# Moving one of three bit steps of the float64 weights, and two small products of the attention, to ScalarE

## The chip, the cores and the metric

The kernel runs on one core of one Trainium2 chip. The metric is the device time of one execution in microseconds, as the median over runs. The engines are called by their names: TensorE (PE in the profile, its weight loads PEld), VectorE (DVE), ScalarE (ACT), GpSimd (POOL) and SyncE (SP, which issues the DMAs).

## The reference

Three parts follow each other: a linear attention with a decaying state, an MLP, and a mixture of experts with one expert per token.

```python
# attention: r, k, v, w (4, 8, 768, 48), u (8, 48)
for t in range(S):
    cur = np.einsum('bhd,bhe->bhde', u[None] * kt, vt)
    y[:, :, t] = np.einsum('bhd,bhde->bhe', rt, state + cur)
    state = wt[:, :, :, None] * state + np.einsum('bhd,bhe->bhde', kt, vt)
# MLP on x (3072, 384): w_in (384, 2048), w_out (2048, 384), both float64
h = x @ w_in
g = np.maximum(h, 0.0) + alpha * np.minimum(h, 0.0)
x = g @ w_out
# experts: argmax of x @ w_gate chooses one of 8
h = np.maximum(xe @ w1[e], 0.0)
out[mask] = gate_w[mask, None] * (h @ w2[e])
```

`w_in` and `w_out` come as float64: a float32 array divided by the square root of a float64 number. The kernel gets them as pairs of 32-bit words and makes float32 of them itself.

## The kernel before

The 3072 tokens are 24 tiles of 128 rows. Three tiles make a block, so there are 8 blocks. For each tile the attention makes `y`, transposed, straight into the MLP's input `xth` (high part) and `xtl` (what the high part leaves). The MLP goes through a block in 16 chunks of 128 of its 2048 columns: `p1` (line 611) multiplies a chunk of `w_in` with the block's `x`, ScalarE makes `gn` (614), VectorE `gt` (616), ScalarE `gh` (622), VectorE `gl` (624), and `p2` (637) multiplies by the chunk of `w_out` two steps later. Every product of the MLP is three matmuls, high by high, high by low and low by high; so each weight exists as `wih` and `wil` (or `woh` and `wol`).

**The weights.** There are 16 pieces, called weight 0 to 15 here; the even ones are of `w_in`, the odd ones of `w_out`, and weights 2g and 2g+1 serve chunks 2g and 2g+1. `wl_stages` makes each in four stages: `rebase` (216), where ScalarE copies the high word, read as a float32, with a scale of 2^-112 into `v64`; `words` (220 to 224), where VectorE shifts that three bits to the left, ors the top three bits of the low word in, and then the sign; `high` (237) on ScalarE and `low` (241) on VectorE. The tiles `raw` and `v64` have two buffers each; weight 2 lies in `spare`. The DMA of weight j+2 is issued on SyncE's queue after `words` of weight j.

**The attention of a tile.** VectorE scans the decays (`ex`, 291) and their inverses backwards (`rec`, 316) and multiplies `k` by them (333); GpSimd multiplies `r` by `ex` (306). TensorE makes the scores `pa` (371), ScalarE copies them to `at` (379), GpSimd masks them (383, two instructions). For the diagonal GpSimd makes `rk` in two products (338, 339), VectorE sums it into `c`, eight numbers per row (344), and GpSimd multiplies `c` with `v` into `cv`, two instructions (351). `cv` has one buffer for all tiles. TensorE transposes it into `px` (438), adds what the state (446, 449) and the scores (459) give, and ScalarE and VectorE make `xth` (464) and `xtl` (469) of it.

**The order.** Everything before the first `p1` is written out by hand: a table gives each step of tiles 0 to 2 and weights 0 to 2 a place (`PRO_OPS`, `PRO_MOVED`, `PRO_W`), and blocks of idle matmuls (`warm`, 161) are set between. From there on TensorE and GpSimd keep the written order, while the order on VectorE and ScalarE is made by a planner when the program is built. On every engine the queue runs strictly in its order: an instruction that waits holds up all behind it. Tiles 0 to 6 use the backward scan (`NBACK`); the attention of tiles 3, 4, 5 lies between the chunks of block 0.

Of the kernel before, what the change touches and what calls it, by code (L numbers as in the profile page):

```python
# [9 lines left out]
F32 = mybir.dt.float32  # L10
F32R = mybir.dt.float32r
BF16 = mybir.dt.bfloat16
I32 = mybir.dt.int32
U32 = mybir.dt.uint32
AF = mybir.ActivationFunctionType
ALU = mybir.AluOpType
AX = mybir.AxisListType
# [3 lines left out]
B, H, S, D = 4, 8, 768, 48  # L21
# [44 lines left out]
NSPE = 7  # L66

NBACK = 7

DMW = 2 * 512 + NP * 129 + 1  # L70

# [36 lines left out]
def attention_mlp_moe(ctx, tc, dmaj, tmaj, ub, alpha, w_in, w_out, w_gate, w_gate_b, wexp, out):  # L108
    nc = tc.nc
    vec, act, pool, pe, sp = nc.vector, nc.scalar, nc.gpsimd, nc.tensor, nc.sync  # L110
# [75 lines left out]
    raw_t, spare_t, wgb_t = {}, {}, {}  # L186
# [5 lines left out]
    def wl_dma(j):  # L192
        g, kind = j // 2, j % 2
        if j == 2:
            raw = spare_t[0][:, 1024:2560].bitcast(U32).rearrange("p (n c) -> p n c", c=2)
        else:
            raw = rp.tile([128, 768, 2], U32, tag="raw", name="raw")
        sp.dma_start(
            out=raw, in_=(w_in if kind == 0 else w_out)[g].bitcast(U32).rearrange("p (n c) -> p n c", c=2)
        )  # L200
# [6 lines left out]

    def wl_stages(j):

        g, kind = j // 2, j % 2  # L210
        q = g % 4
        cx = {}

        def rebase():
            cx["v"] = rp.tile([128, 768], F32, tag="v64", name="v64")
            act.activation(cx["v"], raw_t[j][:, :, 1].bitcast(F32), AF.Copy, scale=2.0**-112)

        def words():
            raw, vu = raw_t.pop(j), cx["v"].bitcast(U32)
            vec.tensor_scalar(vu, vu, 3, None, op0=ALU.logical_shift_left)  # L220
            vec.scalar_tensor_tensor(
                out=vu, in0=raw[:, :, 0], scalar=29, in1=vu, op0=ALU.logical_shift_right, op1=ALU.bitwise_or
            )
            vec.scalar_tensor_tensor(
                out=vu, in0=raw[:, :, 1], scalar=0x80000000, in1=vu, op0=ALU.bitwise_and, op1=ALU.bitwise_or
            )

        def parts():
            if kind == 0:
                sl = (slice(None), slice(None), slice(256 * q, 256 * q + 256))  # L230
                return wi_h[g // 4][sl], wi_l[g // 4][sl], cx["v"].rearrange("p (c f) -> p c f", c=KC)
            sl = (slice(None), slice(2 * q, 2 * q + 2))
            return wo_h[g // 4][sl], wo_l[g // 4][sl], cx["v"].rearrange("p (c d) -> p c d", c=2)

        def high():
            hi, _, v = parts()
            act.copy(hi, v)

        def low():
            hi, lo, v = parts()  # L240
            vec.tensor_tensor(out=lo, in0=v, in1=hi.bitcast(F32), op=ALU.subtract)  # L241

        return rebase, words, high, low

    tri = cst.tile([128, 128], BF16, name="tri")
# [33 lines left out]
    def att_tile(i, s0):  # L279
        cx = {}  # L280
        blk, j = divmod(i, NB)
# [6 lines left out]
        def scan():  # L288
# [13 lines left out]
            cx["v"] = tm_t[i][:, 2 * DM : 3 * DM]  # L302
            cx["rec"] = ap.tile([PR, NP, 129 if i < NBACK else 128], F32, tag="rec", name="rec", bufs=1)

# [3 lines left out]
        def rec(n):  # L308

            def at4(t, m):  # L310
                return t.rearrange("p a (g m) -> p a g m", m=4)[:, :, :, m]

            rc, ex = cx["rec"], cx["ex"][:, :, 1:129]
            if n == 0 and i < NBACK:
                vec.reciprocal(out=inj[:, :, 128], in_=ex[:, :, 127])
# [8 lines left out]
            elif n == 0:  # L324
                vec.reciprocal(out=at4(rc, 3), in_=at4(ex, 3))
            elif n == 1 and i < NBACK:
                return
# [19 lines left out]
        def diag_v():  # L347
            c, v = cx["c"], cx["v"].rearrange("p (a e) -> p a e", a=NP)
            cv = ap.tile([128, DM], F32, tag="cv", name="cv", bufs=1)
            for at, w, out in ((0, 32, cv[:, : 32 * H]), (64, 16, cv[:, 32 * H :])):  # L350
                pool.tensor_tensor(
                    out=out.rearrange("p (a m e) -> p a m e", a=NP, m=2),
                    in0=v[:, :, at : at + 2 * w].rearrange("p a (m e) -> p a m e", m=2),
                    in1=c.rearrange("p (a m o) -> p a m o", a=NP, o=1).to_broadcast([128, NP, 2, w]),
                    op=ALU.mult,
                )
            cx["cv"] = cv

        def decay():
            pm = ap.tile([PR, NP, 96], F32, tag="pm", name="pm", bufs=1)  # L360
            for p in range(NP):
                act.activation(pm[:, p, :], bmask[:, p, :], AF.Copy, scale=cx["ex"][:, p, 128:129])
            cx["pm"] = pm
# [102 lines left out]
        def x_low():  # L466
# [4 lines left out]
        ops = {  # L471
            "scan": scan, "r": decay_r, "rec0": lambda: rec(0), "rec1": lambda: rec(1), "k": lambda: rec(2),
            "rk": diag, "c": diag_sum, "cv": diag_v, "sc": scores,
            "a0": lambda: scores_out(0), "m0": lambda: mask(0), "a1": lambda: scores_out(1), "m1": lambda: mask(1),
            "yst": yst, "yav0": lambda: yav(0), "yav1": lambda: yav(1), "xh": x_out, "xl": x_low,
# [9 lines left out]
    def gate_block(blk, x2, g0):  # L485
# [39 lines left out]
        def bc(t):  # L525
            return t.to_broadcast([128, nt, E])
# [3 lines left out]
        def route():  # L530
# [15 lines left out]
            vec.tensor_tensor(out=sh, in0=l, in1=bc(m), op=ALU.subtract)  # L546
            act.activation(sh, sh, AF.Exp)
            cx.update(sh=sh, mi=mi, oh=oh, ac=ac)
# [53 lines left out]
    def p1(blk, f):  # L602
# [10 lines left out]
        gn = mp.tile([128, BN], F32, tag="gr", name="gn")  # L613
        act.activation(gn, ph, AF.Relu, scale=-1.0)  # L614
        gt = mp.tile([128, BN], F32, tag="gt", name="gt")
# [213 lines left out]
    def u_p1(u, f):  # L829
# [9 lines left out]
        gh = qp.tile([128, UNIT], F32R, tag="gh2", name="gh2", bufs=4)  # L839
        act.activation(gh, ph, AF.Relu)  # L840
        gl = qp.tile([128, UNIT], F32R, tag="gl2", name="gl2", bufs=4)
# [18 lines left out]
    def b_p1(u, q):  # L860
# [10 lines left out]
        hs = qp.tile([128, 256], F32, tag="hs", name="hs")  # L871
        act.activation(hs, ph, AF.Relu)
        d["hs", q] = hs
# [104 lines left out]
    for j in range(NWL):  # L978
        if j < len(PRO_W):
            s = [PT0 + t for t in PRO_W[j]]  # L980
        else:
            s = [2 * j - WL_OFF + n for n in range(4)]
        if j == NWL // 2:
            at_slot(s[0], lambda: w_tiles(1))
        for n, fn in enumerate(wl_stages(j)):
            at_slot(s[n], fn)
        if j and j + 2 < NWL:
            at_slot(s[1], lambda j=j: wl_dma(j + 2))
# [25 lines left out]
    for i in range(len(steps) + LAG):  # L1014
# [7 lines left out]
        if i < len(steps):  # L1022
            kind, b, f = steps[i]
# [6 lines left out]
        if i >= LAG:  # L1030
            kind, b, f = steps[i - LAG]
# [14 lines left out]
    with tc.For_i(0, nrem, 1) as iv:  # L1046
        tb = qp.tile([1, 1, 2], I32, tag="tb", name="tb", bufs=1)
        sp.dma_start(
            out=tb, in_=tabd[:, ds(iv * 2, 2)].rearrange("p (o c) -> p o c", o=1)
# [80 lines left out]
```

## Time and profile before

| | |
|---|---|
| median of 3 runs | 850.45 us (849.12 to 850.51) |
| the profiled execution, its own time | 848.63 us |
| its span, first to last instruction | 846.8 us |
| mean granted clock of TensorE, share of full speed | 0.985 |
| busy: TensorE, VectorE, ScalarE, GpSimd | 800.0, 611.5, 383.1, 306.6 us |

The time of an execution has 1.8 us around the span. Busy times are sums over the whole span and tell little of the first 130 us, where three engines share the attention, the weights and the MLP's first block. A row of the views names the source line, the engine and the operation, then the tile written and the tiles read; "idle before" is the time that the engine stood still ahead of it, and behind the arrow stands what ended that.

### The profile page before, as it was taken

Reading aid. Unit: us, or ns where it says so; the run is one execution under the profiler, and the core shown is the slowest. Engines: PE = TensorE matmul, PEld = TensorE weight load, DVE = VectorE, ACT = ScalarE, POOL = GpSimd, SP = SyncE. Lnnn points to the kernel's source line nnn. Section 1 sums busy time; section 2 is a strip of 40 time slices with the busy share of each in tenths; the row PEclk is TensorE's granted clock in tenths of the full one; section 3 lists DMA queues with packets and bytes.
Section 4 is the critical chain, followed back from the end, with each engine's and each line's share of the span. In section 5 each row is a group of like instructions: output and inputs, shape, how many; then the busy total and the mean of one; then the engine's idle time right before and its main releaser. Section 6 shows DMA issues by size and latency. Waiting matters only on the chain. (4 is left out here: it accounts for less than half of the span.)

```text
span 846.8 us, 15713 instructions
## 1 busy us (share of the span) xinstructions
PE 800.0 (94%) x6032; PEld 752.2 (89%) x6032; DVE 611.5 (72%) x1145; ACT 383.1 (45%) x730; POOL 306.6 (36%) x326
## 2 busy tenths in 40 slices
PE   6777999999999999999999999999899999999994
PEld 4567788999899999899999989989899999999993
DVE  5999995458958968967977953556856676767761
ACT  2465554334334243243343333355446566665641
POOL 6845562343324334334333431130433233223301
PEclk9889999999999999999999999999999999999998
DMA  9825652223123122124123200066277677686820
GB/s 284 256 87 205 216 179 96 66 69 96 38 96 69 63 70 86 46 70 124 35 68 96 67 2 29 2 242 214 95 254 250 216 239 256 229 299 200 297 95 20
DMA packets 30516, 114.80 MB, mean 136 GB/s; under 512 B 8229, under 2 KB 11592, under 8 KB 30440
## 3 DMA queue, kind: packets, MB, share of 16 engines
q1 hardware_dynamic: 26088, 103.53, 37.7%
q0 software_dynamic: 4352, 10.26, 3.2%
q8 instruction: 48, 0.79, 0.4%
q14 instruction: 28, 0.23, 0.1%
HBM read 104.11 MB, written 10.45 MB: 135 GB/s over the span
## 5 line engine op out<-in xcount | busy, mean ns | idle before, releaser
L611 PE MATMUL ph<-xth,wih 128*128 128x384 f32 x384 | 135.7, 353 | 13.6 <-DVE gt L616 10.3
L637 PE MATMUL py<-woh,gh 128*128 128x384 f32 x384 | 134.8, 351 | 1.7 <-DVE x L648 1.7
L611 PE MATMUL ph<-xth,wil 128*128 128x384 f32 x384 | 130.5, 340 | 3.7 <-DVE wil L241 3.7
L611 PE MATMUL ph<-xtl,wih 128*128 128x384 f32 x384 | 129.7, 338 | 0.1
L637 PE MATMUL py<-woh,gl 128*128 128x384 f32 x384 | 129.1, 336 | 0.0
L637 PE MATMUL py<-wol,gh 128*128 128x384 f32 x384 | 128.9, 336 | 0.0
L622 ACT CAST gh<-gt 128x384 fp32r<-128x384 f32 x128 | 65.7, 513 | 138.6 <-DVE gt L616 137.8
L616 DVE SCALAR_TENSOR_TENSOR gt<-gn,oma_s,ph 128x384 f32<-128x384 f32 x128 | 77.8, 608 | 54.6 <-ACT gn L614 54.4
L624 DVE TENSOR_TENSOR gl<-gt,gh 128x384 fp32r<-128x384 f32 x128 | 85.8, 670 | 30.6 <-ACT gh L622 28.3
L614 ACT ACTIVATE gn<-ph 128x384 f32<-128x384 f32 x128 | 62.4, 488 | 83.3 <-PE ph L611 80.1
L842 DVE SCALAR_TENSOR_TENSOR gl<-ph,gh 128x256 fp32r<-128x256 f32 x96 | 40.4, 422 | 73.3 <-ACT gh L840 73.1
L611 PEld LDWEIGHTS ph<-xth,wih 128*128 128x128 f32 x384 | 72.8, 189 | 20.7 <-DVE gt L616 13.0
L383 POOL TENSOR_SCALAR_AFFINE_SELECT at<-at 128x512 f32<-128x512 f32 x46 | 39.8, 884 | 124.0 <-ACT at L379 124.0
L512 DVE SCALAR_TENSOR_TENSOR sink<-x,wgb 128x384 f32<-128x384 f32 x120 | 82.8, 713 | 1.5 <-ACT x L648 1.2
L911 POOL DMA_INDIRECT out<-ys,meta x28 | 28.2, 1009 | 150.7 <-ACT ys L908 93.3
L837 PE MATMUL ph<-xh,w1h 128*128 128x256 f32 x288 | 81.2, 282 | 1.7 <-DVE gl L842 1.6
L837 PE MATMUL ph<-xh,w1l 128*128 128x256 f32 x288 | 80.9, 281 | 0.0
L837 PE MATMUL ph<-xl,w1h 128*128 128x256 f32 x288 | 80.3, 279 | 0.0
L637 PEld LDWEIGHTS py<-woh,gh 128*128 128x128 f32 x384 | 72.4, 189 | 7.9 <-issue 2.8
L611 PEld LDWEIGHTS ph<-xth,wil 128*128 128x128 f32 x384 | 72.9, 190 | 5.2 <-DVE wil L241 5.2
L611 PEld LDWEIGHTS ph<-xtl,wih 128*128 128x128 f32 x384 | 72.9, 190 | 0.4 <-DVE xtl L469 0.4
L637 PEld LDWEIGHTS py<-woh,gl 128*128 128x128 f32 x384 | 72.4, 188 | 0.6 <-DVE gl L624 0.6
(218 smaller groups left out, 1864.2 us busy)
## 6 DMA issues: line engine op xcount, KB each, us to landing
raw<-w SPq DMA_DIRECT2D x64, 768.0 KB, 5.0
tm<-tmaj SPq DMA_DIRECT2D x21, 704.0 KB, 4.3
dm<-dmaj SPq DMA_DIRECT2D x21, 674.2 KB, 4.9
raw<-w_out SPq DMA_DIRECT2D x8, 768.0 KB, 4.3
raw<-w_in SPq DMA_DIRECT2D x7, 768.0 KB, 4.8
x2d<-x SPq DMA_DIRECT2D x8, 576.0 KB, 4.0
both<-tmaj SPq DMA_DIRECT2D x3, 704.0 KB, 9.5
wgb<-w_gate_b SPq DMA_DIRECT2D x2, 768.0 KB, 4.4
```

Source lines behind the costliest of these rows:

```text
L383: pool.affine_select(out=cx[jj], in_=cx[jj], pattern=[[0, NP], [1, 128]], compare_op=ALU.is_gt, fill=0.0, base=0, channel_multiplier=-1,)
L512: vec.scalar_tensor_tensor(out=sink, in0=x2[:, j, :], scalar=1.0, in1=wgb_t[h][:, e, :], op0=ALU.mult, op1=ALU.mult, accum_out=cx["l"][:, ...
L611: pe.matmul(ph, lhsT=w, rhs=x[:, c, :], start=k == 0, stop=k == 3 * KC - 1)
L614: act.activation(gn, ph, AF.Relu, scale=-1.0)
L616: vec.scalar_tensor_tensor(out=gt, in0=gn, scalar=oma_s[:, f : f + 1], in1=ph, op0=ALU.mult, op1=ALU.add)
L622: act.copy(gh, gt)
L624: vec.tensor_tensor(out=gl, in0=gt, in1=gh.bitcast(F32), op=ALU.subtract)
L637: pe.matmul(y_t[blk][j], lhsT=g[:, sl], rhs=w, start=f == 0 and m == 0, stop=f == NF1 - 1 and m == 2,)
L837: pe.matmul(ph, lhsT=w, rhs=x, start=k == 0, stop=k == 3 * KC - 1)
L842: vec.scalar_tensor_tensor(out=gl, in0=ph, scalar=0.0, in1=gh.bitcast(F32), op0=ALU.max, op1=ALU.subtract)
L911: pool.indirect_dma_start(out=out, out_offset=bass.IndirectOffsetOnAxis(ap=d["meta"][:, j, 0:1], axis=0), in_=ys, in_offset=None, bounds_c ...
```

## The change

Two things move to ScalarE. First, `rebase` gets a second activation: it reads the top byte b of each low word (byte 3 of 8, in steps of 8 bytes) and writes (b − 15.5) / 32, rounded to an integer, over the low word; that is the word's top three bits. `words` loses its first instruction, the shift, and takes the shift into the instruction that ors the three bits in. Second, for tiles 1 and 2 `cv` is made by ScalarE, one activation per head with `c` of that head as scale, 16 per tile, instead of two instructions on GpSimd.

```diff
+CVACT = (1, 2)
...
         def rebase():
             cx["v"] = rp.tile([128, 768], F32, tag="v64", name="v64")
-            act.activation(cx["v"], raw_t[j][:, :, 1].bitcast(F32), AF.Copy, scale=2.0**-112)
+            raw = raw_t[j]
+            act.activation(cx["v"], raw[:, :, 1].bitcast(F32), AF.Copy, scale=2.0**-112)
+            byte = raw.rearrange("p n c -> p (n c)").bitcast(U8).rearrange("p (n b) -> p n b", b=8)[:, :, 3]
+            act.activation(raw[:, :, 0], byte, AF.Copy, scale=2.0**-5, bias=-15.5 * 2.0**-5)
 
         def words():
             raw, vu = raw_t.pop(j), cx["v"].bitcast(U32)
-            vec.tensor_scalar(vu, vu, 3, None, op0=ALU.logical_shift_left)
             vec.scalar_tensor_tensor(
-                out=vu, in0=raw[:, :, 0], scalar=29, in1=vu, op0=ALU.logical_shift_right, op1=ALU.bitwise_or
+                out=vu, in0=vu, scalar=3, in1=raw[:, :, 0], op0=ALU.logical_shift_left, op1=ALU.bitwise_or
             )
...
             for at, w, out in ((0, 32, cv[:, : 32 * H]), (64, 16, cv[:, 32 * H :])):
+                if i in CVACT:
+                    for h in range(H):
+                        act.activation(
+                            out[:, w * h : w * h + w],
+                            v[:, h // 2, at + w * (h % 2) : at + w * (h % 2) + w],
+                            AF.Copy,
+                            scale=c[:, h : h + 1],
+                        )
+                    continue
                 pool.tensor_tensor(
```

The line numbers in the changed kernel are up to 17 higher. The planner makes the order on VectorE and ScalarE anew, so more moves than the diff says. On ScalarE in the prologue (`cv_338` and `cv_395` are tile 1's and tile 2's, `raw_152` and `v64_417` belong to weight 1) the changed program has, between the copies of tile 2's scores and weight 0's high part:

```order
L396 COPY at1_334<-pa1_314 128x512
L418 COPY kt_336<-pk_327 128x448
L361 ACTIVATE cv_338<-both_144,c_269 128x32 x8
L361 ACTIVATE cv_338<-both_144,c_269 128x16 x8
L361 ACTIVATE cv_395<-both_147,c_393 128x32 x8
L361 ACTIVATE cv_395<-both_147,c_393 128x16 x8
L223 ACTIVATE v64_417<-raw_152 128x768
L225 ACTIVATE raw_152<-raw_152 128x768
L245 CAST wih0_122<-v64_323 128x3x256
```

Before, weight 1's activation and weight 0's high part stood right behind `kt`; now all 32 activations of `cv` are ahead of them.

On VectorE, around weight 8 (`v64_743` before, `v64_771` now; its low part `wil1` is what chunk 8 needs first), the program had before, with chunk 6's and chunk 7's `gt`:

```order
L616 SCALAR_TENSOR_TENSOR gt_776<-gn_774,oma_s_110,ph_764 128x384
L221 SCALAR_TENSOR_TENSOR v64_743<-raw_671,v64_743 128x768
L624 TENSOR_TENSOR gl_798<-gt_776,gh_796 128x384
L224 SCALAR_TENSOR_TENSOR v64_743<-raw_671,v64_743 128x768
L220 TENSOR_SCALAR v64_779<-v64_779 128x768
L616 SCALAR_TENSOR_TENSOR gt_842<-gn_840,oma_s_110,ph_830 128x384
L221 SCALAR_TENSOR_TENSOR v64_779<-raw_719,v64_779 128x768
L241 TENSOR_TENSOR wil1_740<-v64_743,wih1_739 128x3x256
```

and the changed program has, from chunk 5's `gt` on:

```order
L633 SCALAR_TENSOR_TENSOR gt_764<-gn_762,oma_s_110,ph_752 128x384
L229 SCALAR_TENSOR_TENSOR v64_771<-v64_771,raw_699 128x768
L641 TENSOR_TENSOR gl_776<-gt_764,gh_774 128x384
L249 TENSOR_TENSOR wol0_125<-v64_728,woh0_124 128x768
L232 SCALAR_TENSOR_TENSOR v64_771<-raw_699,v64_771 128x768
L633 SCALAR_TENSOR_TENSOR gt_804<-gn_802,oma_s_110,ph_792 128x384
L352 TENSOR_REDUCE c_1075<-rk_927 128x8
L249 TENSOR_TENSOR wil1_768<-v64_771,wih1_767 128x3x256
```

`wil1` has moved from behind chunk 7's `gt` to behind chunk 6's, and the sum `c` of tile 5, which came after it, stands ahead of it.

On VectorE, around chunk 11 (`gt_1069` is its `gt`, `gl_1092` its `gl`; `c_1304` is tile 6's), the changed program has:

```order
L633 SCALAR_TENSOR_TENSOR gt_1069<-gn_1067,oma_s_110,ph_1057 128x384
L232 SCALAR_TENSOR_TENSOR v64_1034<-raw_946,v64_1034 128x768
L341 TENSOR_TENSOR dm_1009<-dm_1009,rec_1132 112x512
L352 TENSOR_REDUCE c_1304<-rk_1205 128x8
L229 SCALAR_TENSOR_TENSOR v64_1072<-v64_1072,raw_1016 128x768
L249 TENSOR_TENSOR wol1_770<-v64_1034,woh1_769 128x768
L641 TENSOR_TENSOR gl_1092<-gt_1069,gh_1090 128x384
L232 SCALAR_TENSOR_TENSOR v64_1072<-raw_1016,v64_1072 128x768
L633 SCALAR_TENSOR_TENSOR gt_1124<-gn_1122,oma_s_110,ph_1112 128x384
L633 SCALAR_TENSOR_TENSOR gt_1162<-gn_1160,oma_s_110,ph_1150 128x384
L249 TENSOR_TENSOR wil1_768<-v64_1072,wih1_767 128x3x256
```

Before, that `c` came after chunk 15's `gt`; now it stands ahead of chunk 11's `gl`. `c` of tile 4 has moved in the same way, from behind chunk 5's `gl` to behind weight 4's `wil`, ahead of chunk 2's `gl`.

## Rows read from the trace of the kernel before

**Rows 1.** TensorE's waits, 38 to 160 us: who waited for whom, total, times, longest.

```profile
PE ph L611 <- DVE gt L616: 6.0, 1, 6.0
PE ph L611 <- DVE wil L241: 3.7, 4, 2.0
PE ph L611 <- ACT wih L237: 3.3, 2, 1.8
```

**Rows 2.** Busy time by stretch; last: granted clock, DMA share, GB/s.

```profile
28.00:30.00 2.00, 1.61 (x9) 0.99 (x11) 2.00 (x3) 0.97 (x2) 1.39 (x2) 0.50 0.98 220
43.50:49.50 6.00, 0.01 (x1) 0.00 (x0) 6.00 (x10) 3.41 (x8) 2.99 (x2) 0.82 0.00 1
77.50:82.00 4.50, 0.73 (x4) 0.33 (x3) 4.50 (x7) 2.28 (x4) 4.50 (x4) 0.95 0.50 167
82.00:84.40 2.40, 2.40 (x8) 2.38 (x9) 2.40 (x2) 0.59 (x1) 2.40 (x2) 0.50 0.04 15
```

**Rows 3.** Instruction groups, VectorE, 22 to 125 us: count, busy us, mean ns, idle before.

```profile
L224 DVE SCALAR_TENSOR_TENSOR v<-raw,v 128x768 uint32<-128x768 uint32 x15 | 16.3, 1089 | 0.1
...
L220 DVE TENSOR_SCALAR v<-v 128x768 uint32<-128x768 uint32 x16 | 10.2, 640 | 0.2 <-ACT v L216 0.2
```

**Rows 4.** Instruction groups, ScalarE, 20 to 125 us.

```profile
L216 ACT ACTIVATE v<-raw 128x768 f32<-128x768 f32 x15 | 13.7, 914 | 8.8 <-DMA raw<-w_out 5.7 <-DVE v L220 2.3 <-DVE wil L241 0.8
...
L362 ACT ACTIVATE pm<-bmask,ex 112x96 f32<-112x96 bf16 x20 | 6.0, 368 | 0.0
```

**Rows 5.** Order of time, ScalarE: start us, us, instruction, count, idle before.

```profile
26.79 0.55 ACT L401 COPY kt<-pk 128x448 f32<-128x448 f32 x1
...
146.06 0.22 ACT L547 ACTIVATE g_sh<-g_sh 128x24 f32<-128x24 f32 x1 [1.73 <-DVE g_sh L546]
```

**Rows 6.** Order of time, GpSimd, prologue and the chains of four tiles.

```profile
26.57 2.40 POOL L351 TENSOR_TENSOR cv<-both,c 128x256 f32<-128x256 f32 x2
29.59 2.94 POOL L351 TENSOR_TENSOR cv<-both,c 128x256 f32<-128x256 f32 x2 [0.61 <-PE px L438]
...
50.81 1.98 POOL L383 TENSOR_SCALAR_AFFINE_SELECT at<-at 128x512 f32<-128x512 f32 x2 [3.99 <-ACT at L379]
...
56.01 1.61 POOL L339 TENSOR_TENSOR rk<-rk,ub_s 128x384 f32<-128x384 f32 x1
...
101.70 6.68 POOL L383 TENSOR_SCALAR_AFFINE_SELECT at<-at 128x512 f32<-128x512 f32 x2 [6.67 <-ACT at L379]
...
130.10 1.00 POOL L339 TENSOR_TENSOR rk<-rk,ub_s 128x384 f32<-128x384 f32 x1
...
152.43 1.22 POOL L383 TENSOR_SCALAR_AFFINE_SELECT at<-at 128x512 f32<-128x512 f32 x2 [4.01 <-ACT at L379]
153.63 1.19 POOL L306 TENSOR_TENSOR dm<-dm,ex 112x512 f32<-112x512 f32 x1
```

**Rows 7.** Order of time, TensorE, the five places of the sum.

```profile
29.03 0.48 PE L438 MATMUL px<-ident,cv 128*128 128x128 f32 x1 [0.39 <-POOL cv L351]
...
38.37 0.48 PE L611 MATMUL ph<-xth,wih 128*128 128x384 f32 x1
...
81.97 0.69 PE L611 MATMUL ph<-xth,wil 128*128 128x384 f32 x1 [1.96 <-DVE wil L241]
...
108.94 0.33 PE L637 MATMUL py<-woh,gl 128*128 128x384 f32 x1
...
113.01 0.44 PE L611 MATMUL ph<-xth,wil 128*128 128x384 f32 x1 [0.44 <-DVE wil L241]
```

**Rows 8.** Order of time, VectorE, the chain to the first gt.

```profile
31.74 0.53 DVE L220 TENSOR_SCALAR v<-v 128x768 uint32<-128x768 uint32 x1
...
37.69 0.56 DVE L469 TENSOR_TENSOR xtl<-px,xth 128x384 fp32r<-128x384 f32 x1
...
48.89 0.60 DVE L616 SCALAR_TENSOR_TENSOR gt<-gn,oma_s,ph 128x384 f32<-128x384 f32 x1
```

**Rows 9.** The mask instructions of line 383: ns min/median/max.

```profile
L383 POOL TENSOR_SCALAR_AFFINE_SELECT at<-at x24: 624/635/6098, 32.5 to 286.1; 128x512 f32<-128x512 f32 x24
```

More of the change, by code (lines that the diff above doesn't have):

```diff
@@ L14 @@
 U32 = mybir.dt.uint32
+U8 = mybir.dt.uint8
 AF = mybir.ActivationFunctionType
```

## Prediction

> **What bounds the kernel now.** TensorE does the work, so I first read its waits between 38 and 160 us, where the change acts. It waits 6.0 us once for `gt`, 3.7 us in four pieces for the low halves `wil`, and 3.3 us in two for the high halves `wih` [rows 1]: 13.0 us, nearly all behind VectorE, because `wih` in turn waits for VectorE's last pass over the words. The busy times by stretch say the same: while TensorE stands still at 43.5 to 49.5 and at 77.5 to 82.0, VectorE is busy for all of it, 6.00 and 4.50 us, and ScalarE for about half [rows 2]. A stall also costs afterwards: after both, the granted clock is 0.50, the lower level of 1.2 GHz (82.0 to 84.4) [rows 2]. Later the first layer runs at TensorE's own pace, so what the start gains or loses reaches the end one to one.
>
> So the question is whether VectorE, relieved of an instruction per weight, passes its relief on to TensorE, or stops for another engine. I follow five places of TensorE [rows 7]: the third transpose of tile 1's `cv` (29.03), the first matmul of the MLP (38.37), the first `wil` matmul of chunk 8 (81.97), the first `gl` matmul of chunk 11 in the second layer (108.94), and the first `wil` matmul of chunk 14 (113.01). Any shift left at the last one is the forecast.
>
> **What is removed and added.** Sixteen shifts leave VectorE, 10.2 us [rows 3]. Each of the two remaining passes keeps its form: two SBUF sources, 768 elements, 1.09 us as the row of L224 has it [rows 3]. ScalarE gets 16 byte activations. Their nearest row is the float one over the same 768 places in steps of 8 bytes, 914 ns [rows 4], of which about 0.8 occupies the queue; 14.6 us in all, on an engine that is half idle. Bounds: 0.8, and twice that if bytes went at half the rate; I take 0.8, because partitions, count and steps are equal.
>
> Per weight the swap loses 914 − 640 = 0.27 us of engine time, 4.4 us over 16 [rows 3, 4]; only one weight or two lie on the chain in the stretches above, and the sum has them below. The rule in the Trainium skill ("ScalarE: Activation LUTs", Rules for kernel authors) is to put multiplies and adds on VectorE, not ScalarE; by it the whole of that would be lost, and the sum would be 855 instead of 852.5 (last rival).
>
> GpSimd loses two pairs of `cv`, 2.40 and 2.94 us [rows 6]; ScalarE gets 32 small activations with a per-partition scale. The trace has that form at 96 elements, 368 ns each [rows 4], four in 1.18 us, thus 0.27 per instruction in the queue; a plain one of 24 elements lasts 0.22 us [rows 5], 0.13 if it overlaps likewise. For 16 and 32 elements I take 0.21, nearest the first row as it also has the scale: 3.4 us a tile, bounds 2.1 and 4.3.
>
> **Start of the MLP.** ScalarE reaches tile 1's `cv` behind `kt`, which ends at 27.3 [rows 5]; sixteen activations end at 30.65, so the third transpose moves from 29.03 to 30.65. From there to 38.37 TensorE had no idle time, part of it at clock 0.50 [rows 2]; it moves along by 1.6 us.
>
> Queued behind `cv` on ScalarE is weight 1. The `cv` buffer is single: tile 2's `cv` waits for tile 1's transposes (31.1) and ends at 34.5. Weight 1's two activations follow until 36.2. VectorE began on that weight at 31.74 [rows 8] and now stands idle until 36.2. Two passes, the first `wil`, an `xtl` and a product later (0.9, 0.9, 0.9, 0.5, 0.6), it reaches the last `xtl` at 39.9 instead of 37.69. From there to the first `gt` it took 11.2 us [rows 8]. Out of this go three shifts (2.1) and one pass (0.9); in come the backward scan and the product of tile 4 (1.7), now placed earlier, and a longer wait for ScalarE (0.25): 10.1 us, `gt` at 50.0 instead of 48.89. **Shift +1.1** (−0.4 to +3.1 by the bounds on `cv` and on the byte activation). The 5 us that VectorE stood idle have eaten the first shifts' relief.
>
> **Chunk 8.** Between that `gt` and `wil` of weight 8, VectorE has 3.9 us less to do (out: five shifts 3.2, scan and product 1.7, a `gt`, `gl` and a pass of weight 9 together 2.2; in: a pass of weight 3, scan and product of tile 5, `c` of tile 5, together 3.2). But `c` of tiles 4 and 5 now stand in its queue ahead of them. Each needs GpSimd's chain: two masks, `r` product, two `rk` products, begun by ScalarE's copies of the scores. That chain took 50.81 to 57.62, 6.8 us, under a busy VectorE, and its undisturbed parts sum to 1.22 + 1.19 + 2 x 1.00 = 4.4 [rows 6]. For tile 4 it starts at 51.6 to 53.3, so `c` comes at about 59 and stops VectorE for some 2 us, which TensorE does not feel yet. For tile 5 the copies end at 76, VectorE arrives at `c` at 77.5 to 79, and the chain ends between 80 and 82.2. I take 81.5: `c` 0.5 and `wil` 0.9 bring chunk 8 to 82.8 instead of 81.97. **Shift +0.8**, −0.6 to +2.5. TensorE's stall there stays, under another name, with its low clock.
>
> **Chunks 11 to 14.** From 81.97 to 108.94 TensorE needed 27.0 us, of which two stalls on weight 12 made 2.1; these go, as weight 12 comes about 2 us ahead of need. So it asks for chunk 11's `gl` at 107.7. VectorE has `c` of tile 6 in front of that `gl`, with the first pass of weight 14 and a `wol` between. The copies of tile 5's scores end at 102.5, masks and products need 4.4 to 6.8 us again: `c` ends at 108.3, `gl` 2.25 us later at 110.55. TensorE waits 2.9 us. Then 4.07 us less a stall of 0.44 [rows 7] take it to chunk 14: 114.2; if the clock falls after that wait, up to 1.7 us more, of which I take half: 115.0 instead of 113.01. **Shift +2.0**, −3.4 to +6.8 with all ends.
>
> The sum is thus 848.63 + 2.0 = 850.6 us for an execution like the profiled one. That one is 1.8 us below the median of the runs, 850.45; on this scale **852.5 us**. A measurement here tells about 0.2%, 1.7 us, from no change.
>
> **The rivals.** *VectorE's relief gets through.* It decides whether GpSimd has finished `rk` of tile 6 when VectorE reaches `c` (about 105). If each chain takes its 4.4 us and the waits at `c` vanish, chunk 8 comes 0.6 us earlier and the stalls on weights 12 and 14 go without a successor: 0.6 + 2.1 + 0.44, and 0.3 of early start, −3.4, **847.1 us**. For it: VectorE is the bound, and 10.2 us leave it. Against: the chain takes 6.8 us whenever VectorE is busy.
>
> *GpSimd starves.* One mask, 635 ns in the median, lasted 6098 [rows 9]: the pair begun at 101.70 took 6.68 us [rows 6], under a VectorE that was never idle. If the chains of tiles 5 and 6 move only once VectorE stops, chunk 8 comes at 84.5, `gl` 29.4 us after it, the clock falls, and chunk 14 is late by 6 us: **856.5 us**. For it: that row; against: at 50.81 the same two masks took 1.98. The Trainium skill ("SBUF — State Buffer", on the shared port pair) states that VectorE with two SBUF inputs and GpSimd exclude each other for a whole instruction; the mask's row agrees.
>
> *ScalarE becomes the long leg.* If every weight waits for its second activation, the 0.27 us of each lie on the chain: +4.4, **855 us**. A byte activation of twice 0.8 us would come to the same: weights 1 and 2 reach VectorE 1.6 us later each. Against it: ScalarE idles half of the time where TensorE waits [rows 2], and no row shows a byte source.
>
> **How the numbers follow.** Forecast (shift −0.7 to +3.8) 0.50, relief 0.20, starvation 0.25, ScalarE 0.05. Faster by over 0.2%: most of the relief case and a little of the forecast, 0.20. Within 0.2%, 848.75 to 852.15: somewhat over half of the forecast and a rest of the relief, 0.32. Slower: 0.48. The range 847 to 857 leaves out half of the relief case (0.10) and the upper tail of the slow ones (0.08); the forecast's own is 849.7 to 854.3.
>
> **What would show it.** In the new profile: the third transpose of tile 1 near 30.6; a VectorE idle of about 5 us before weight 1 and the first `gt` near 50; VectorE's wait for `rk` several us where it is now under one; chunk 8's `wil` matmul near 82.8 with TensorE waiting for `wil`; no wait at weight 12, but one of about 3 us for `gl` of chunk 11; chunk 14 near 115. I am wrong if TensorE's waits between 38 and 160 sum to under 11 us, or if chunk 14 comes before 112; a byte activation far from 914 ns speaks for the third rival.

## The result, and the profile after

The changed kernel took 856.5 us (median of 7 runs, 852.79 to 857.38) beside 850.51 us for the kernel before on the same chip: a ratio of 1.006, 95% interval 1.0038 to 1.0082. It is slower, by more than the 0.2% that a measurement can tell, and the time lies above the 852.5 us forecast; the range of 847 to 857 just holds it. A later set of runs of the same program gave 855.43 us and a ratio of 1.0049 (1.0031 to 1.0068). The loss is thus 4 to 6 us.

| | before | after, first profile | after, second profile |
|---|---|---|---|
| span, us | 846.8 | 855.5 | 852.4 |
| granted clock of TensorE | 0.985 | 0.976 | 0.979 |
| busy VectorE, ScalarE, GpSimd, us | 611.5, 383.1, 306.6 | 599.4, 400.9, 282.4 | 597.2, 400.5, 283.7 |

VectorE was relieved of 12 to 14 us and the time rose. TensorE's waits of the first profile, 38 to 160 us (who waited for whom, total, times, longest), against [rows 1]:

```profile
PE ph L628 <- DVE gt L633: 6.5, 2, 6.0
PE py L654 <- DVE gl L641: 4.4, 1, 4.4
PE ph L628 <- DVE wil L249: 3.6, 1, 3.6
PE py L654 <- DVE x L665: 1.0, 1, 1.0
PE ph L628 <- ACT wih L245: 0.7, 1, 0.7
```

The 3.3 us for `wih` have shrunk to 0.7, and a wait of 4.4 us for one `gl` has come. Four of the places of [rows 7], in order of time, TensorE, first profile:

```profile
34.12 0.48 PE L455 MATMUL px<-ident,cv 128*128 128x128 f32 x1 [1.26 <-ACT cv L361]
...
88.53 0.69 PE L628 MATMUL ph<-xth,wil 128*128 128x384 f32 x1 [3.65 <-DVE wil L249]
...
118.73 0.69 PE L654 MATMUL py<-woh,gl 128*128 128x384 f32 x1 [4.37 <-DVE gl L641]
...
123.79 0.35 PE L628 MATMUL ph<-xth,wil 128*128 128x384 f32 x1
```

and in the second profile:

```profile
30.84 0.47 PE L455 MATMUL px<-ident,cv 128*128 128x128 f32 x1 [1.11 <-ACT cv L361]
...
84.71 0.69 PE L628 MATMUL ph<-xth,wil 128*128 128x384 f32 x1 [3.65 <-DVE wil L249]
...
114.60 0.69 PE L654 MATMUL py<-woh,gl 128*128 128x384 f32 x1 [4.37 <-DVE gl L641]
...
119.55 0.34 PE L628 MATMUL ph<-xth,wil 128*128 128x384 f32 x1
```

The two differ by 3.8 us at chunk 8 and by 4.1 at chunk 11, but these two waits are the same to 0.01 us. What differs lies ahead of the MLP, and the change doesn't cause it: in the first, `c` of tile 1 starts at 20.28 instead of 18.67, and one scan of tile 2 takes 4.24 us instead of 2.17 (last section). In the profile of before, `c` of tile 1 starts at 18.69. So the second profile is the one to set against before, and the comparison below uses it.

VectorE there (order of time, idle before in brackets): its wait for weight 1, the scan and the product of tile 4, the first `gt`, and `c` of tiles 5 and 6.

```profile
36.34 0.96 DVE L229 SCALAR_TENSOR_TENSOR v<-v,raw 128x768 uint32<-128x768 uint32 x1 [5.41 <-ACT raw L225]
...
47.68 1.44 DVE L324 TENSOR_TENSOR_SCAN rec<-dm,inj 112x516 f32<-112x516 f32 x1
...
49.89 0.89 DVE L341 TENSOR_TENSOR dm<-dm,rec 112x512 f32<-112x512 f32 x1
50.70 0.60 DVE L633 SCALAR_TENSOR_TENSOR gt<-gn,oma_s,ph 128x384 f32<-128x384 f32 x1
...
83.24 0.55 DVE L352 TENSOR_REDUCE c<-rk 128x8 f32<-128x384 f32 x1 [3.19 <-POOL rk L347]
83.71 0.95 DVE L249 TENSOR_TENSOR wil<-v,wih 128x768 fp32r<-128x768 f32 x1
...
111.79 0.55 DVE L352 TENSOR_REDUCE c<-rk 128x8 f32<-128x384 f32 x1 [1.96 <-POOL rk L347]
...
114.00 0.55 DVE L641 TENSOR_TENSOR gl<-gt,gh 128x384 fp32r<-128x384 f32 x1
```

Behind each `c` stands what TensorE waits for: `wil` at 83.71 for the matmul at 84.71, `gl` at 114.00 for the one at 114.60. In all, VectorE waits 10.9 us for `rk` between 20 and 140 us, where it was 4.0 before. At `c` of tiles 4 to 6 alone it is 8.3 us against 0.8; a large part of the relief has gone there. GpSimd's chains for the two (order of time):

```profile
77.69 2.32 POOL L400 TENSOR_SCALAR_AFFINE_SELECT at<-at 128x512 f32<-128x512 f32 x2 [13.02 <-ACT at L396]
79.98 1.18 POOL L314 TENSOR_TENSOR dm<-dm,ex 112x512 f32<-112x512 f32 x1
81.13 1.00 POOL L346 TENSOR_TENSOR rk<-tm 128x384 f32<-128x384 f32 x1
82.20 1.00 POOL L347 TENSOR_TENSOR rk<-rk,ub_s 128x384 f32<-128x384 f32 x1
...
105.03 2.30 POOL L400 TENSOR_SCALAR_AFFINE_SELECT at<-at 128x512 f32<-128x512 f32 x2 [11.82 <-ACT at L396]
107.30 1.98 POOL L314 TENSOR_TENSOR dm<-dm,ex 112x512 f32<-112x512 f32 x1
109.24 1.45 POOL L346 TENSOR_TENSOR rk<-tm 128x384 f32<-128x384 f32 x1
110.77 0.99 POOL L347 TENSOR_TENSOR rk<-rk,ub_s 128x384 f32<-128x384 f32 x1
```

They take 5.5 and 6.7 us, from the first mask, which follows ScalarE's first copy of the scores, to the end of `rk`. Last, busy time by stretch (TensorE first; behind the five engines the granted clock), over the path from the first `gt` to chunk 8, chunk 11 and chunk 14, of the kernel before:

```profile
49.55:81.97 32.42, 28.00 (x192) 25.18 (x192) 31.78 (x43) 19.51 (x37) 15.27 (x10) 0.92 0.55 189
81.97:108.94 26.97, 24.88 (x177) 22.16 (x177) 26.17 (x37) 15.12 (x28) 17.87 (x8) 0.95 0.61 201
108.94:113.01 4.07, 3.63 (x45) 2.74 (x44) 4.07 (x7) 2.64 (x5) 4.07 (x2) 1.00 0.28 92
```

and of the second profile of the change:

```profile
51.36:84.71 33.35, 28.21 (x191) 25.28 (x192) 26.82 (x38) 23.21 (x42) 16.89 (x12) 0.91 0.54 185
84.71:114.60 29.89, 25.52 (x176) 23.13 (x176) 25.60 (x35) 19.84 (x34) 7.63 (x7) 0.90 0.53 179
114.60:119.55 4.95, 4.95 (x44) 4.21 (x45) 4.95 (x8) 2.91 (x5) 1.68 (x1) 0.70 0.47 162
```

The start is 1.81 us late (51.36 against 49.55), and the stretches are 0.93, 2.92 and 0.88 longer: 6.54 us at chunk 14, 5.6 of which are left in the span. In the stretches TensorE stands still 2.56 us longer in all, and is busy 2.17 us longer with the same matmuls, at a lower granted clock (0.70 for 1.00 in the last). These differences are of two single executions. The one of the kernel before (848.63 us) lies 3.1 us under that kernel's median in the later set (851.75), the one of the change 1.3 us under its own (855.43); so some 1.8 of the 5.6 us come from the pair that was profiled.

### The profile page after: what moved, and what is told of

It reads as the page before. It is cut to its first block, busy times and chain, and to the rows that moved or that the text cites. A ratio compares the mean times of both kernels' runs of the same rounds, so it can differ in the third digit from the quotient of the medians.

```text
span 855.5 us, 15743 instructions
## 1 busy us (share of the span) xinstructions
PE 805.8 (94%) x6032; PEld 758.1 (89%) x6032; DVE 599.4 (70%) x1129; ACT 400.9 (47%) x778; POOL 282.4 (33%) x322
## 5 line engine op out<-in xcount | busy, mean ns | idle before, releaser
L628 PE MATMUL ph<-xth,wih 128*128 128x384 f32 x384 | 135.5, 353 | 11.4 <-DVE gt L633 10.7
L641 DVE TENSOR_TENSOR gl<-gt,gh 128x384 fp32r<-128x384 f32 x128 | 83.9, 655 | 31.7 <-ACT gh L639 29.4
L400 POOL TENSOR_SCALAR_AFFINE_SELECT at<-at 128x512 f32<-128x512 f32 x46 | 37.3, 830 | 155.1 <-ACT at L396 155.1
L654 PEld LDWEIGHTS py<-wol,gh 128*128 128x128 f32 x384 | 73.1, 190 | 0.0
```

The source lines that it names most:

```text
L400: pool.affine_select(out=cx[jj], in_=cx[jj], pattern=[[0, NP], [1, 128]], compare_op=ALU.is_gt, fill=0.0, base=0, channel_multiplier=-1,)
L628: pe.matmul(ph, lhsT=w, rhs=x[:, c, :], start=k == 0, stop=k == 3 * KC - 1)
L641: vec.tensor_tensor(out=gl, in0=gt, in1=gh.bitcast(F32), op=ALU.subtract)
L654: pe.matmul(y_t[blk][j], lhsT=g[:, sl], rhs=w, start=f == 0 and m == 0, stop=f == NF1 - 1 and m == 2,)
```

## The experiments

Three theories were set against each other; the expectations call some of them by letter. **A**: in the order that the planner makes of the change, `c` stands ahead of `gl` and `wil` on VectorE and waits there for GpSimd's `rk`. **B**: the loss is made in the prologue, where ScalarE has two `cv` ahead of weight 1 and the start is delayed. **C**: the byte activation itself costs too much. A ratio is against the kernel before, with runs of the same set; the interval is 95%.

**Each half alone.** The byte step without `cv`, in the changed kernel:

```diff
-CVACT = (1, 2)
+CVACT = ()
```

> The change without its second half: cv of tiles 1 and 2 stays on GpSimd. Theory A (two causes: cv ahead of weight 1 on ScalarE delays the start of the MLP, and the sum c of tiles 4 to 6, now ahead of the weights and of gl in VectorE's queue, waits for GpSimd): the third transpose of tile 1 is back near 29 us and the first gt before 49.5, but VectorE's waits for rk stay at 6 us or more and TensorE still waits 2 us or more for gl of chunk 11; time 850 to 853 us, ratio 1.000 to 1.003. Theory B (cv alone costs, the bit step pays): VectorE's relief reaches TensorE, 845 to 848 us, ratio 0.994 to 0.997. Theory C (ScalarE's sixteen further activations are the long leg): 853 us or more, ratio above 1.003, with VectorE waiting for L225 several us in all.

And `cv` without the byte step: the kernel before with the change's `CVACT` and its loop of activations.

```diff
+CVACT = (1, 2)
...
+                if i in CVACT:
+                    for h in range(H):
+                        act.activation(
...
+                    continue
```

> The second half alone: cv of tiles 1 and 2 on ScalarE, the shift stays on VectorE. Theory A: the third transpose near 31 us or later, VectorE idle 4 us or more before weight 1, first gt 2 us or more later than 48.89; no wait for gl of chunk 11 and VectorE's waits for rk near 1 us, since c stands late as before; time 852 to 855 us, ratio 1.002 to 1.005. Theory B: the whole loss of the change or more, 856 to 860 us, ratio 1.006 to 1.010. Theory C: as before, 850 us, ratio 1.000.

Measured: 851.87 us, 1.0011 (0.9991 to 1.0031), and 852.72 us, 1.0004 (0.9986 to 1.0022). Neither half alone can be told from no change. The profiled execution of the byte step shows the change's waits nearly whole, 11.4 us for `rk`, TensorE's 3.8 for `gl` and 3.7 for `wil`; but with a span of 853.1 it lies 3 us above that kernel's median, so it can't speak for the median. Its first `gt` was expected before 49.5 us; it came at 51.86, 32.1 us after `c` of tile 1, as late as in the change (32.0). With `cv` alone VectorE waits 3.2 us for `rk` and 2.7 for weight 1 (4 or more expected), and the first `gt` comes 30.3 us after `c` of tile 1, as before (30.2), although the third transpose is about as late as in the change (12.0 us after that `c`; 12.2 in the change, 10.3 before). Theory C has little left here: with the byte step alone VectorE waits 1.6 us for byte activations between 20 and 140 us, and all 15 of them between 20 and 125 us take 909 ns in the mean, as the plain ones do (ScalarE's groups, here from the second profile of the change):

```profile
L223 ACT ACTIVATE v<-raw 128x768 f32<-128x768 f32 x15 | 13.7, 911 | 8.3 <-DVE wol L249 3.6 <-DMA raw<-w_out 3.0 <-DVE wil L249 1.3
L225 ACT ACTIVATE raw<-raw 128x768 uint32<-128x768 uint8 x15 | 13.6, 909 | 0.0
```

**The chain on GpSimd shortened.** The changed kernel, with `rk` of tiles 5 and later ahead of the masks and of `r` in GpSimd's order, so that `c` needs only the tile's own transfer:

```diff
+RKFIRST = {"r": -8, "rk": -10}
+MASK2 = {"m0": 2, "m1": 2}
...
-                at_slot(s0 + OPS[n], fn)
+                at_slot(s0 + (RKFIRST if i > 4 else {}).get(n, (MASK2 if i > 3 else {}).get(n, OPS[n])), fn)
```

> The changed kernel with one thing moved: from tile 5 on GpSimd makes the two products rk of a tile ahead of the masks of the tile before and of the product of r, so that c finds rk done. Theory A: VectorE's waits for rk fall from 9.2 us to 4 or less (tile 4 keeps its own), TensorE's wait for gl of chunk 11 (4.4 us) and most of that for wil of chunk 8 (3.6) go, while the start of the MLP stays late; 5 us less than the changed kernel, 850 to 853 us, ratio 1.000 to 1.003. Theories B and C: the waits at c are not what TensorE feels, or something else takes their place: 855 to 857 us, ratio 1.005 to 1.008.

Measured: 852.52 us, 1.0028 (1.0008 to 1.0048), its median 2.9 us under the change's second one. VectorE doesn't wait for `c` of tiles 5 and 6 any more (order of time; the row at 82.61 stands where the change had 83.24):

```profile
82.08 0.60 DVE L635 SCALAR_TENSOR_TENSOR gt<-gn,oma_s,ph 128x384 f32<-128x384 f32 x1
82.61 0.54 DVE L354 TENSOR_REDUCE c<-rk 128x8 f32<-128x384 f32 x1
83.07 0.95 DVE L251 TENSOR_TENSOR wil<-v,wih 128x768 fp32r<-128x768 f32 x1
...
109.74 0.54 DVE L354 TENSOR_REDUCE c<-rk 128x8 f32<-128x384 f32 x1
...
112.46 0.54 DVE L643 TENSOR_TENSOR gl<-gt,gh 128x384 fp32r<-128x384 f32 x1
```

and TensorE's waits, 38 to 160 us, are

```profile
PE ph L630 <- DVE gt L635: 7.2, 3, 6.0
PE py L656 <- DVE gl L643: 2.6, 2, 2.3
PE ph L630 <- ACT wih L247: 2.0, 1, 2.0
PE ph L630 <- DVE wil L251: 0.4, 1, 0.4
```

A wait of 2.34 us for `gl` of chunk 11 is left, though `c` finds `rk` done: VectorE has no idle time there, with `c`, a pass of weight 14 and a `wol` ahead of that `gl`. So about half of the change's 4.37 us is the wait for `rk`; the rest is VectorE's own work, which in the new order stands ahead of that `gl`.

From the first `gt` to the `gl` twenty chunks later this execution needs 95.0 us, the change 98.8 and the kernel before 95.5. That this is all the work of the waits at `c` is not shown: with `cv` alone, where `c` of tiles 4 to 6 waits as little as before and no `gl` keeps TensorE waiting, the same path took 98.5 us, with a granted clock of 0.77 from 86 to 90 us and of 0.64 from 114 to 118 where it was 1.00 before. Theory A is right in that the waits for `rk` hold TensorE up and that the edit takes them away. What that is worth is less certain: 2.9 us by the medians, 0.2% or some 2 us by the ratios, whose intervals overlap.

**The same edit without the change, and with the byte step alone.** In the kernel before (same lines):

> The kernel before, with the one edit of the run that put the rk products of tiles 5 and later ahead of the masks and r of the next tiles in GpSimd's order. It asks whether that edit is worth something by itself, or only undoes what the change did. Theory A (the change's loss is c waiting for rk ahead of gl and wil; in the kernel before VectorE hardly waits there): ratio within 0.2% of 1, VectorE's waits for rk already under 1.5 us, TensorE's stall for wil at chunk 8 still about 3.5 us. Rival (the order on GpSimd costs the kernel before too, and the change has nothing to do with it): ratio 0.997 or lower, by the same 0.3% that the edit gave the changed kernel.

In the changed kernel without `cv` on ScalarE (same lines, and `CVACT = ()`):

> The byte step alone (cv of tiles 1 and 2 stays on GpSimd) with rk of tiles 5 and later ahead on GpSimd. If the loss has two parts, the later c (removed by the order on GpSimd) and the longer prologue (removed by leaving cv on GpSimd), nothing of it is left and VectorE's ten us of relief show: ratio 0.996 to 0.999, TensorE's waits between 38 and 160 us under 11 us, first gt near 51 to 52, no wait for gl of chunk 11 over 2 us. If the byte step costs something of its own on ScalarE, the ratio stays at 1.001 or above, with VectorE waiting for ScalarE's v by 2 us or more past weight 2.

Measured: 851.35 us, 0.9986 (0.9968 to 1.0005), and 850.89 us, 0.9978 (0.9961 to 0.9996). The edit is hardly worth anything to the kernel before, as theory A has it, though 0.14% can't be told from none. Nor can it be told from the 0.2% that it gave the change and the 0.3% that it gives the byte step alone (0.9978 against 1.0011), so the rival isn't ruled out by the times. And the kernel before did wait for `rk`, 4.0 us, 3.2 of them at `c` of tile 7; the edit takes these away, while TensorE's waits for `wil` rise from 3.7 to 5.3 us. With the byte step alone the loss is gone, but there it couldn't be told from none without the edit either. The expected fall of TensorE's waits to under 11 us did not come, they sum to 15.4, with 2.3 for `gl` of chunk 11; the first `gt` at 51.83 was as expected. Between this kernel and the one with `cv` on ScalarE too the ratios put 0.5% and the medians 0.2%: with the chain shortened, the two `cv` still cost something beside the byte step, where without the byte step they cost nothing measurable.

**The prologue.** Weight 1's two activations between the two `cv` instead of behind both:

```diff
-PRO_W = ((15.75, 17, 20.5, 20.6), (19.64, 19.65, 24.3, 24.4), (24.2, 24.3, 100, 101))
+PRO_W = ((15.75, 17, 20.5, 20.6), (19.54, 19.65, 24.3, 24.4), (24.2, 24.3, 100, 101))
```

> The changed kernel with weight 1's two activations on ScalarE between cv of tile 1 and cv of tile 2. Theory A: VectorE's idle time before weight 1 falls from 5.9 us to about 3, the first gt comes 1.5 to 3 us earlier than 54.5, cv of tile 2 is not felt as TensorE reaches its transposes later anyway; the waits at c stay; 854 to 855.5 us, ratio 1.004 to 1.005. If the order on ScalarE in the prologue does not matter (the late start is the transfers' and GpSimd's doing): first gt unchanged, 856 to 857 us, ratio 1.006 to 1.007.

Tile 2's `cv` back on GpSimd:

```diff
-CVACT = (1, 2)
+CVACT = (1,)
```

> The changed kernel with cv of tile 2 back on GpSimd; only tile 1's stays on ScalarE. VectorE's order is as in the changed kernel but for one place before the first gt. If the two cv in front of weight 1 on ScalarE make the loss: VectorE's wait for weight 1 falls from 5.4 us to between 1 and 2.5 (3.4 us of ScalarE and its wait for tile 1's transposes go), the first gt is 31 to 31.5 us after c of tile 1, the ratio 1.001 to 1.003. If it is the place of c alone: ratio 1.005 as before, with all the later stalls.

And weights 0 to 4 back to three passes, `cv` and the later byte steps as in the change:

```diff
 def rebase():
...
+            if j < 5:
+                return
...
 def words():
...
+            if j < 5:
+                vec.tensor_scalar(vu, vu, 3, None, op0=ALU.logical_shift_left)
+                vec.scalar_tensor_tensor(
+                    out=vu, in0=raw[:, :, 0], scalar=29, in1=vu, op0=ALU.logical_shift_right, op1=ALU.bitwise_or
+                )
+            else:
```

> The changed kernel, but weights 0 to 4 keep the three passes on VectorE; cv of tiles 1 and 2 on ScalarE, and the byte step from weight 5 on. Each half alone lay within 0.15% of the kernel before, both together 0.5% above it. If both together cost because they meet in ScalarE's queue in the prologue (two cv, then two activations for weight 1, while VectorE waits 5.4 us): VectorE's wait for weight 1 falls to 2.5 to 3 us as with cv alone, the first gt comes 30 to 30.5 us after c of tile 1 instead of 32, and the ratio falls to 1.000 to 1.002. If the loss is made later, by c ahead of gl with the byte step: the ratio stays at 1.004 or above, with the stall for gl of chunk 11 at 4 us.

Measured: 856.41 us, 1.0053 (1.0028 to 1.0078); 855.49 us, 1.0027 (1.0007 to 1.0047); 855.24 us, 1.0039 (1.0016 to 1.0061). The first takes VectorE's wait for weight 1 away and gains nothing: a wait of 1.8 us for `xth` comes in its place, and the first `gt` is 33.5 us after `c` of tile 1 (the change: 32.0). The second only moves the wait, 3.2 us for `xth`, with the `gt` at 32.3. ScalarE isn't what is late there: it stands idle for 3.0 and 4.2 us ahead of that `xth` until TensorE has made its `px` (second run, order of time, ScalarE).

```profile
40.84 0.48 ACT L481 CAST xth<-px 128x384 fp32r<-128x384 f32 x1 [4.24 <-PE px L476]
```

TensorE in turn has no idle time between the third transpose of tile 1 and the first matmul of the MLP (32.19 to 42.03 us in the second run, 30.84 to 40.24 in the change). So a second chain, from `cv` of tile 1 through TensorE's work on tile 2, ends about as late as the one through weight 1, and relieving weight 1 alone gains nothing. The third has the first `gt` 33.3 us after `c`, 2.1 of them a scan of 4.25 us, thus 31.2 without that; its wait for weight 1 is 3.4 us; and it still has 4.42 us for `gl` of chunk 11. None of these three brings back more than about half of the loss by the ratios, and the intervals overlap the change's. Leaving both `cv` on GpSimd, the byte step alone above, brings back more (1.0011 against 1.0049), though its profiled execution has the late start and the waits at `c` of the change. What makes its other executions faster than the change's is seen in no trace and stays open. How the 1.8 us of the start divide between `cv` and the byte step stays open: with `cv` alone the first `gt` comes 30.3 us after `c` of tile 1, with the byte step alone 32.1, and there 2.3 us of VectorE's waits are for a transfer of `dm`.

**`c` placed later.**

```diff
-    "scan": -9, "r": -9, "rec0": -7, "rec1": -5, "k": -3, "rk": -6, "c": 0, "cv": 0, "sc": 0,
+    "scan": -9, "r": -9, "rec0": -7, "rec1": -5, "k": -3, "rk": -6, "c": 3, "cv": 3, "sc": 0,
```

> The changed kernel with one edit of the table of due slots: c and cv become due three slots later. VectorE's order then has c of tile 5 behind the first low half of weight 8 instead of ahead of it; c of tile 6 keeps its place ahead of gl of chunk 11, and GpSimd's order is as in the changed kernel. If the wait at c of tile 5 is what delays chunk 8 (theory A): TensorE's 3.65 us stall for wil there falls to under 2, and the ratio from 1.005 to about 1.003, the stall for gl of chunk 11 remaining at 3 to 5 us. If c only waits because VectorE has time to spare there (rival): the stall at chunk 8 keeps its length under another name, and the ratio stays at 1.005 or above.

Measured: 862.36 us, 1.0123 (1.0093 to 1.0154), far slower than either theory said. One half of the expectation was met, TensorE's wait at chunk 8 fell from 3.65 to 1.91 us. But GpSimd's order was not as in the changed kernel: `cv` took the place that its new due slot gave it, between the masks and `rk` of the next tile (order of time, GpSimd).

```profile
78.67 2.32 POOL L400 TENSOR_SCALAR_AFFINE_SELECT at<-at 128x512 f32<-128x512 f32 x2 [16.91 <-ACT at L396]
80.95 1.18 POOL L314 TENSOR_TENSOR dm<-dm,ex 112x512 f32<-112x512 f32 x1
82.10 0.97 POOL L368 TENSOR_TENSOR cv<-tm,c 128x256 f32<-128x256 f32 x2
83.03 1.71 POOL L346 TENSOR_TENSOR rk<-tm 128x384 f32<-128x384 f32 x1
84.83 1.01 POOL L347 TENSOR_TENSOR rk<-rk,ub_s 128x384 f32<-128x384 f32 x1
```

So `c` of tile 5 came at 85.87 (83.24 in the change), the wait for `gl` of chunk 11 grew to 4.7 us, and new ones of about 1 us came between. It lengthened the chain that theory A is about, and doesn't test `c`'s place alone. By the `gl` twenty chunks after the first `gt` it is 3.6 us behind the change; by the MLP's last `gl` it is 8.3 behind, as at the end of the span (8.2), and what loses the rest in between was not traced.

**A version at least as fast as both.** The byte step from weight 5 on only (the third diff of the prologue), `cv` on GpSimd, `rk` first:

> As the run before, but weights 0 to 4 keep the three passes on VectorE, so that the planner again puts the first gt ahead of the scan and product of tile 4; from weight 5 on ScalarE makes the three bits. If what is left of the loss sits in the start of the MLP (first gt at 51 to 54 where the kernel before has 48.9): first gt at 48.5 to 50, the stall for wil at chunk 8 shorter by 1 to 2 us, ratio 0.995 to 0.998, the fastest version of all. If VectorE's relief of 0.64 us a weight is lost elsewhere anyway (late transfers, the low clock): within 0.2% of the kernel before.

Measured again, and the change once more beside it:

> The version with three passes for weights 0 to 4, the byte step from weight 5 on, cv on GpSimd and rk ahead, measured a second time; nothing edited. It read 0.9979 [0.9961, 0.9998] the first time. If it is truly faster: again under 1, 0.997 to 0.999. If that was the luck of one set of runs: 0.999 to 1.001.

> The changed kernel once more, nothing edited, beside the three kernels below. In its first profile the backward scan of tile 2 lasted 4.24 us, against about 2.1 to 2.2 us in every other profile so far, and the first gt began at 54.5. If that long scan was an accident of one execution: 2.2 us here, the first gt between 50.5 and 53, the ratio near 1.005 with the span 853 to 854. If the changed order itself makes it (VectorE's scan beside GpSimd's r, masks and rk of tile 1): 4.2 us again, the first gt at 54 or later, span 855. Under both, VectorE waits for rk of tiles 4, 5 and 6 about 8 to 10 us in all and TensorE for gl of chunk 11 about 4 us.

It took 850.21 us, 0.9979 (0.9961 to 0.9998), and the second time 850.28 us, 0.9984 (0.9964 to 1.0004). It is clearly faster than the change, and by 0.2% faster than the kernel before, at the edge of what can be told: the second interval includes 1. By the ratios it is no faster than the byte step alone with `rk` first (0.9978). Its first `gt` comes 30.2 us after `c` of tile 1, as in the kernel before, and TensorE's waits, 38 to 160 us, begin with

```profile
PE ph L638 <- DVE gt L643: 8.0, 3, 6.6
PE py L664 <- DVE gl L651: 2.9, 2, 2.3
```

The stall at the start stays, and with it the granted clock of 0.50 behind it. The change's own second profile is the one used above.

## Why the prediction was right in direction and too small

The forecast case, that VectorE's relief is lost in waits for others, is what happened; its size, +2.0 us at chunk 14, was +6.5 in an execution in which `c` of tile 1 starts as before. Both medians of the change, 856.5 and 855.43, lie above 854.3, the upper end of that case; the range held them by the share given to the slow rivals, so the number was right by the width of the range and not by its sum.

- **Prices of the new work: right.** A byte activation as a plain one (909 against 911 ns), `cv` 3.39 us a tile (3.4 forecast).
- **The start: nearly right.** Third transpose at 30.84 (30.65 forecast), VectorE idle 5.41 us ahead of weight 1 (about 5), last `xtl` at 40.14 (39.9), first `gt` at 50.70 (50.0). The first matmul of the MLP is at 40.24, 1.9 later than before (1.6 forecast). Of the 0.7 too little in the `gt`, 0.2 lie ahead of the last `xtl`; the rest is the scan and the product of tile 4, for which the working had 1.7 us and which held VectorE for 2.17 (47.68 to 49.04, 49.89 to 50.70), with GpSimd at `cv`. The wait for weight 2's byte activation, 1.02 us, is as in the working: 0.75 of waits in that stretch before, and 0.25.
- **Chunk 8: place and cause right, size off.** "`c` 0.5 and `wil` 0.9 bring chunk 8 to 82.8": it came at 84.71. The chain took 5.5 us, just as in the sum, but the masks began at 77.69, behind a first copy of the scores that ended at 77.62, not at 76. Of these 1.6 us 0.7 are from the start. Another 0.8 arose on ScalarE: TensorE had the scores ready at 74.19, 1.9 later than before (72.27), but the copies followed them at 77.04 instead of 74.31, because a `woh` ahead of them in the queue waited 1.24 us for VectorE's last pass over a weight. The sum had moved the copies with the start alone.
- **Chunk 11: the step that failed most.** Forecast was a wait of 2.9 us for `gl`, against 2.1 saved at weight 12. The saving came. The wait was 4.37 us: from the copies to the end of the chain it took 6.7 us, close to the upper bound of 6.8, where 5.3 stood in the sum. And TensorE needed 0.64 us more for the same matmuls: the longer wait at chunk 8 is followed by the lower clock, as before, but the sum had no such term there.
- **Chunk 14:** 4.95 us from the `gl` matmul, 4.5 forecast; the clock was 0.70 on average, and of the 1.7 us that the working gave as the price of a fallen clock 1.3 were paid (4.95 less the 3.63 busy before), not half.

Each shift erred to the same side, in part because they aren't independent: a later start made later scores and a later `c` (0.7 us of chunk 8's 1.9), and behind each longer wait the granted clock was at 0.50 for a while (84.4 to 87.0 and 114.6 to 117.0 us). The prediction also read VectorE's wait for `rk` as under one microsecond; that holds for tiles 4 to 6 (0.80), while tile 7's `c` already waited 3.2. The starvation rival gave 856.5 us with chunk 8 at 84.5 and `gl` 29.4 us behind; the measured 84.71 and 29.89 are these numbers, but not its mechanism: no mask of line 400 took over 2.47 us (6.10 before), and both chains moved, if slowly, while VectorE was busy. The relief case fell at its own test, VectorE arrived at `c` of tile 6 at 109.8, 2 us ahead of `rk`.

## What to carry to other kernels

Taking work from the busiest engine pays only if what it does next is ready: look in the new order for an instruction that moves ahead and waits for a slower partner, and shorten that partner's chain first. A planner that remakes the order can put a wait in the place of the relief, so compare the order ahead of each instruction that the bound engine waits for. Shifts along such a chain add up with the same sign; a range around their sum should lean to that side.

## What the runs showed of the hardware

One scan of VectorE took 4.24 us in the first profile of the change and 2.17 in the second, with GpSimd's product begun 0.17 us ahead of it both times. First profile (VectorE's scan, then GpSimd's rows beside it):

```profile
22.22 4.24 DVE L324 TENSOR_TENSOR_SCAN rec<-both,inj 112x516 f32<-112x516 f32 x1
```

```profile
22.05 1.19 POOL L314 TENSOR_TENSOR both<-both,ex 112x512 f32<-112x512 f32 x1 [1.80 <-DVE ex L299]
23.18 1.23 POOL L400 TENSOR_SCALAR_AFFINE_SELECT spare<-spare 128x512 f32<-128x512 f32 x2
24.37 1.00 POOL L346 TENSOR_TENSOR rk<-both 128x384 f32<-128x384 f32 x1
25.46 1.80 POOL L347 TENSOR_TENSOR rk<-rk,ub_s 128x384 f32<-128x384 f32 x1
```

Four instructions of GpSimd ran at their own pace; the scan ended 1.09 us after the fourth of them (25.37), and only the fifth was stretched. In the second profile the masks took the 2.22 us and the scan went ahead of them. That fits whole instructions excluding each other, as the Trainium skill ("SBUF — State Buffer", Who interferes with whom) has it; but the page lets issue order decide who blocks, and here equal order went either way. Four of the fourteen profiles show 4.24 or 4.25 us, of kernels with and without the change. Together with the start of `c` of tile 1, which lies between 17.95 and 20.98 us in them, it makes the runs of one kernel differ by several us, and a single pair of profiles a poor measure of a change of 0.5%.
